# A new order of attention's steps, one softmax inverse a unit, and other places for the experts' first steps, in a fused attention and two-expert kernel

## The chip, the cores and the metric

The kernel runs on one core of a Trainium2 chip. The metric is the device time of one execution in microseconds. Three runs of the kernel before gave 928.98 us at the median (927.47 to 929.08).

## The reference, cut

Window attention over 4 batches, 8 heads, 576 positions and 64 columns a head, then two dense experts on 2304 rows of 512 columns.

```python
def _attn_ref(q, k, v):                         # (4, 8, 576, 64) each, float32
    scores = scale * np.matmul(q, k.transpose(0, 1, 3, 2))
    bias = slopes[:, None, None] * (-np.abs(rel).astype(np.float32))[None, :, :]
    mask = (rel >= 0) & (rel < window)          # window = 128
    scores = np.where(mask, scores + bias[None], -1000000000.0)
    scores = scores - np.max(scores, axis=-1, keepdims=True)
    attn = np.exp(scores)
    attn = attn / (np.sum(attn, axis=-1, keepdims=True) + 1e-09)
    return np.matmul(attn, v).astype(np.float32)

def _moe_ref(x, w_in, w_out, a, b):             # w_in (512, 2048), w_out (2048, 512)
    h = x @ w_in
    P = a[0] + a[1] * h + a[2] * h2 + a[3] * h3
    Q = 1.0 + np.abs(b[0]) * np.abs(h) + np.abs(b[1]) * h2
    return ((P / (Q + 1e-6)) @ w_out).astype(np.float32)

def _moe2_ref(x, w_in, w_out):
    h = x @ w_in
    return (np.where(h > 0.0, h, np.exp(np.minimum(h, 0.0)) - 1.0) @ w_out).astype(np.float32)
```

The weights of both experts come as 8-byte floats and are put together on the chip from their two 32-bit words.

## The kernel before, in words

**Units.** Attention runs over 16 units, `units[u] = (b, p)` with u = 4p + b: a batch b and a pair of heads p (e = 0, 1). A unit's 576 positions are four blocks of 128 and a tail of 64. Its work is cut into named steps:

- `qT`, `kT`, `zT`: TensorE transposes of q, of k and of the two tails; `qC`, `kC`, `zC`: their copies out of PSUM (`qC` on ScalarE, the others on VectorE).
- `S0` to `S4`: the scores on TensorE, five PSUM tiles a unit, taken in turn from three banks. `D0` to `D8`: nine VectorE instructions that add the bias and find the row's extreme. `E0` to `E8`: nine exponentials on ScalarE with the row's sum. `R0` and `R1`: the inverse of the sums (an add and a reciprocal each, over 5 and over 4 of the nine columns, line 523). `N0` to `N8`: the multiplication by the inverse on GpSimd.
- `T00`, `T10`, `T11`, `T01`: transposes of the probabilities, `C..` their copies on ScalarE. `V0`, `V1`, `Y`: the product with v. `XC` and `XY`: the copies of the result (128x512 and 128x64) into `xT`.
- `s`, `a`, `b`, `h`, `l` with 0 or 1: a weight's conversion, two weights in each of units 3 to 14 (`PLAN`, line 32): a scale on ScalarE, then a shift, a joining of the words, and the high and the low part on VectorE.

**The order.** `STEPS` (line 18) is a table written out by hand: each row is a step and how many iterations it runs ahead of (or behind) the loop's count t. The loop at line 667 goes through the table once an iteration and issues step by step, so the table sets the order on all engines' queues. Each engine runs its queue in order. A step that writes a buffer waits for the buffer's last readers. After the table's last row, three early iterations build the bias of the next head pair (`biases`, line 388, four VectorE instructions).

**The end of attention.** At iteration 15 `split_x` (line 217) splits the first 384 rows of `xT` into a high and a low part. From there on steps of the first expert stand between attention's: `early()` (line 264) gives the first products of the first four chunks (`gemm1`, 48 matmuls of 128x384, three at each `next`), at the places that `AHEAD` (line 34) names, and what is left runs after attention; `CONV_AFTER` (line 33) names six places for a step of the conversion of four more weights; `FIRST` (line 41) names where the elementwise part of chunks 0 and 1 stands (`rational`, line 269). The first product into the output accumulators (`gemm2_T(0)`, line 699) needs `ghi` and `glo` of chunk 0, which VectorE makes at lines 295 to 313.

**After attention** the first expert runs 96 chunks, each a `gemm1` and a `gemm2_T`, then the second expert. Nothing of that is changed.

## Time and profile before

| what | us |
| --- | --- |
| median of three runs (lowest, highest) | 928.98 (927.47, 929.08) |
| the profiled execution, its own time | 929.59 |
| its span, first to last instruction | 927.8 |
| busy: TensorE matmul, VectorE, ScalarE, GpSimd | 915.4, 795.9, 737.1, 185.0 |
| attention's unit in the middle of attention | 8.44 |
| first `gemm2_T` matmul that reads `glo`, from the span's start | 155.36 |

Times are read from the span's start. A timeline row has the start and the duration of an instruction (or of several in a row), its engine, line and tiles, and in brackets how long the engine stood idle before it and what ended that. On one engine the next row can begin before the last has ended, since instructions overlap at their ends; so what an instruction costs its engine is the distance from its start to the next start. Matmuls are pipelined, so a busy TensorE need not be at its peak.

### The profile page before, as it was taken

The page shows a single profiled execution, that of the slowest core. Times are in us where ns is not written, and L with a number is a line of the kernel's source. Part 1 is how long each engine was busy: PE and PEld are TensorE (multiplying, and loading weights), DVE is VectorE, ACT ScalarE, POOL GpSimd, SP SyncE. Part 2 cuts the span into 40 slices and gives each one's busy share as a digit, 9 for nine tenths or more (in the row PEclk, how much of TensorE's full clock was granted, in tenths as well). Part 3 has the DMA queues.
Part 4 walks back from the last instruction along what each step waited for, and adds up shares of the span by engine and source line. Part 5 has one row for each costly group of instructions (what it writes and reads, how often), then busy time and mean ns, then how long its engine had stood idle before and what let it go on. Part 6 is the DMA issues. An engine that isn't in the chain of part 4 may idle for free.

```text
span 927.8 us, 16722 instructions
## 1 busy us (share of the span) xinstructions
PE 915.4 (99%) x5494; PEld 839.2 (90%) x5494; DVE 795.9 (86%) x1873; ACT 737.1 (79%) x1614; POOL 185.0 (20%) x260
## 2 busy tenths in 40 slices
PE   8999999999999999999999999999999999999998
PEld 5776778999999999999999998888989898988887
DVE  6899999998998998998989999999978688677653
ACT  6999997889888888889888987676776567767553
POOL 5666661122222222222222210000000000000000
PEclk9999999999999999999999999999999999999999
DMA  8899952011222222222200034445253323442201
GB/s 160 228 247 240 222 168 82 1 35 58 85 80 70 86 69 86 85 63 92 85 31 29 3 119 136 164 144 197 80 170 103 121 83 98 142 148 81 79 0 69
DMA packets 112567, 98.35 MB, mean 106 GB/s; under 512 B 62816, under 2 KB 86368, under 8 KB 112480
## 3 DMA queue, kind: packets, MB, share of 16 engines
q1 hardware_dynamic: 109936, 96.57, 35.4%
q10 hardware_dynamic: 2544, 0.72, 0.4%
q8 instruction: 43, 0.70, 0.3%
q14 instruction: 44, 0.36, 0.1%
HBM read 79.96 MB, written 17.30 MB: 105 GB/s over the span
## 4 chain that ended last, share of the span: by engine, by line
PE 79%; DVE 15%; DMA 2%; ACT 2%; issue 2%; DVEq 0%; ACTq 0%; SPq 0%
PE acc L932 21%; PE m L916 18%; PE acc L708 18%; PE h L254 18%; DVE pr_wi L502 1%; DVE cvt L146 1%; PE s_ps L476 1%; DVE pr_wo L502 1%; PE x L569 1%; DMA v<-in_v_dram 1%; DVE w_wi L160 1%; DVE qq L298 1%; DVE ghi L295 1%; DVE ee L316 1%; DVE qkT L445 1%
## 5 line engine op out<-in xcount | busy, mean ns | idle before, releaser
L254 PE MATMUL h<-xs,w_wi 128*128 128x384 f32 x1152 | 216.9, 335 | 0.3 <-DVE xs L227 0.2
L254 PEld LDWEIGHTS h<-xs,w_wi 128*128 128x128 f32 x1152 | 200.7, 188 | 1.6 <-DVE xs L230 0.7
L708 PE MATMUL acc<-ghi,w_wo 128*128 128x384 f32 x768 | 194.8, 334 | 0.0
L313 POOL TENSOR_TENSOR glo<-ee,rr 128x384 fp32r<-128x384 f32 x92 | 93.6, 1018 | 311.3 <-DVE ee L312 109.3
L708 PEld LDWEIGHTS acc<-ghi,w_wo 128*128 128x128 f32 x768 | 138.6, 188 | 0.3 <-issue 0.3
L708 PE MATMUL acc<-glo,w_wo 128*128 128x384 f32 x384 | 128.4, 334 | 1.1 <-DVE glo L313 1.1
L932 PE MATMUL acc<-op_wo,ghi 128*128 128x512 f32 x288 | 89.6, 392 | 0.0
L916 PE MATMUL m<-xo_wi,op_wi 128*128 128x384 f32 x336 | 77.2, 337 | 0.0
L916 PE MATMUL m<-xo_wo,op_wi 128*128 128x384 f32 x336 | 76.5, 335 | 0.0
L301 ACT ACTIVATE rr<-qq,c_q 128x384 f32<-128x384 f32 x96 | 59.1, 616 | 18.6 <-DVE qq L298 17.7
L708 PEld LDWEIGHTS acc<-glo,w_wo 128*128 128x128 f32 x384 | 72.1, 188 | 1.4 <-DVE glo L313 1.4
L978 ACT ACTIVATE oo<-qq 128x384 f32<-128x384 f32 x24 | 12.6, 524 | 73.8 <-DVE qq L972 73.8
L284 ACT ACTIVATE oo<-h,a_sb 128x384 f32<-128x384 f32 x96 | 67.9, 707 | 3.4 <-DVE h L315 3.2
L287 ACT ACTIVATE ee<-h,a_sb 128x384 f32<-128x384 f32 x96 | 67.6, 704 | 0.0
L298 DVE SCALAR_TENSOR_TENSOR qq<-h,b_abs,qa 128x384 f32<-128x384 f32 x92 | 56.1, 609 | 12.4 <-ACT qa L283 11.3
L916 PEld LDWEIGHTS m<-xo_wo,op_wi 128*128 128x128 f32 x336 | 60.8, 188 | 4.0
L295 DVE TENSOR_TENSOR ghi<-ee,rr 128x384 fp32r<-128x384 f32 x96 | 53.5, 557 | 12.2 <-ACT h L282 0.5
L316 DVE TENSOR_TENSOR ee<-ee,h 128x384 f32<-128x384 f32 x96 | 53.3, 555 | 10.4 <-DVE h L315 0.5
L932 PEld LDWEIGHTS acc<-op_wo,ghi 128*128 128x128 f32 x288 | 53.5, 188 | 8.9
L916 PEld LDWEIGHTS m<-xo_wi,op_wi 128*128 128x128 f32 x336 | 60.5, 188 | 0.0
L282 ACT ACTIVATE h<-h 128x384 f32<-128x384 f32 x96 | 46.3, 482 | 15.2 <-PE h L254 14.5
L972 DVE TENSOR_TENSOR ee<-ee,m 128x384 f32<-128x384 f32 x96 | 52.7, 549 | 5.1 <-PE m L916 4.9
(184 smaller groups left out, 2067.6 us busy)
## 6 DMA issues: line engine op xcount, KB each, us to landing
pair<-joined_wo SPq DMA_DIRECT2D x43, 256.0 KB, 2.6
raw_wo<-in_moe_w_out_dram SPq DMA_DIRECT2D x20, 512.0 KB, 4.8
raw_wi<-in_moe_w_in_dram SPq DMA_DIRECT2D x16, 512.0 KB, 4.4
half<-in_moe_w_in_dram SPq DMA_DIRECT2D x32, 256.0 KB, 2.7
two_wo<-joined_wi SPq DMA_DIRECT2D x32, 256.0 KB, 2.9
s<-sums SPq DMA_DIRECT2D x32, 256.0 KB, 2.7
half<-in_moe_w_out_dram SPq DMA_DIRECT2D x22, 256.0 KB, 2.8
v<-in_v_dram SPq DMA_DIRECT2D x32, 128.0 KB, 3.4
```

The source lines that it names most:

```text
L254: nc.tensor.matmul(h, lhsT=WT["wi", f][:, SEL[wp], kk * P:(kk + 1) * P], rhs=x[xp][kk], start=(kk == 0 and n == 0), stop=(kk == KD - 1 and ...
L284: nc.scalar.activation(out=oo, in_=h2, func=AF.Identity, scale=a_sb[:, 3:4], bias=a_sb[:, 1:2])
L287: nc.scalar.activation(out=ee, in_=h2, func=AF.Identity, scale=a_sb[:, 2:3], bias=a_sb[:, 0:1])
L295: nc.vector.tensor_tensor(out=hi, in0=ee0, in1=rr0, op=ALU.mult)
L298: nc.vector.scalar_tensor_tensor(out=qq, in0=h2, scalar=b_abs[:, 1:2], in1=qa, op0=ALU.mult, op1=ALU.add)
L301: nc.scalar.activation(out=rr, in_=qq, func=AF.Ln, bias=c_q)
L313: (nc.gpsimd if c > 4 else nc.vector).tensor_tensor(out=low, in0=ee0, in1=rr0, op=ALU.mult)
L316: nc.vector.tensor_tensor(out=ee, in0=ee, in1=h, op=ALU.add)
L708: nc.tensor.matmul(acc_t[d], lhsT=WT["wo", f][:, SEL[wp], d * P:(d + 1) * P], rhs=gt[SEL[xp]], start=(f == 0 and n == 0), stop=(f == KF - ...
L916: nc.tensor.matmul(out, lhsT=w[:, SEL[wp], c0:c0 + P], rhs=XO[q // NP2, nm, k][:, SEL[xp]], start=(k == 0 and n == 0), stop=(k == 1 and n ...
L932: nc.tensor.matmul(acc_t[T, t], lhsT=gt[SEL[xp]][:, t * P:(t + 1) * P], rhs=w[:, SEL[wp]], start=(first and n == 0), stop=(last and n == 2),)
L972: nc.vector.tensor_tensor(out=t, in0=R[q, x], in1=M[q, m], op=ALU.add)
```

## The change

1. `STEPS` is a new table: all steps stand in another order and with other leads. One `R` over all nine columns takes the place of `R0` and `R1`.
2. `x_copy` becomes two steps: `XC` copies on ScalarE when u is even, `XD` on VectorE when u is odd (and for the last three units, as before).
3. The loads of q, k and v of a later unit are issued when all steps that read the buffer have been issued, whichever is last.
4. `AT_END` takes the place of `AHEAD`, `CONV_AFTER` and `FIRST`: it lists after which step of which unit each first step of the expert stands: `xA`/`xD` the split of x, `g0` to `g7` six matmuls of `gemm1` each, `r0a` to `r1d` the parts of the elementwise work of chunks 0 and 1 (`first_rational`), `zs`, `za`, `zb`, `zh`, `zl` with 0 to 3 the conversion steps of four more weights.

```diff
 STEPS = (
-    ("T00", -1), ("a0", 1), ("l1", -1), ("C01", -1), ("S0", 1), ("S1", 1), ("C00", -1),
...
+    ("qT", 3), ("E2", 1), ("D3", 2), ("XC", -1), ("T11", 0), ("h0", 1), ("C10", 0), ("h1", 0),
...
+    ("b1", 1), ("E0", 2), ("C00", 1), ("T10", 1), ("XD", 0), ("N7", 1), ("D1", 3),
 )
+AT_END = {
+    ("E5", 15): "xA xD",
+    ("T11", 14): "g0",
+    ("T01", 14): "g1",
+    ("C01", 14): "zs0 r0a",
+    ("V1", 14): "g2",
+    ("XY", 14): "r0b",
+    ("T10", 15): "g3",
+    ("XD", 14): "r0d za0 za2 zb0 za3 zh0",
+    ("T01", 15): "g4",
+    ("C01", 15): "r1a",
+    ("V1", 15): "g5 g6 g7",
+    ("XY", 15): "zl0 r1b zs3 r1c r0c zs2 zs1",
+    ("XD", 15): "zb3 zh3 r1d zl3 za1 zb1 zb2 zh2 zh1 zl2 zl1",
+}
...
-CONV_AFTER = ((15, "E8"), (15, "R1"), (14, "V1"), (15, "T01"), (15, "T11"), (15, "V1"))
-AHEAD = {
-    (14, "T00"): 1, (14, "T10"): 1, (14, "T11"): 2, (14, "V0"): 1, (14, "V1"): 2, (14, "Y"): 1,
-}
...
-FIRST = {"r0": (14, "Y"), "r1": (15, "C11")}
...
+    def first_rational(c):
...
+        def a():
+            nc.scalar.activation(out=h2, in_=h, func=AF.Square)
+            nc.scalar.activation(out=qq, in_=h, func=AF.Abs, scale=b_abs[:, 0:1])
+            nc.scalar.activation(out=oo, in_=h2, func=AF.Identity, scale=a_sb[:, 3:4], bias=a_sb[:, 1:2])
+            nc.scalar.activation(out=ee, in_=h2, func=AF.Identity, scale=a_sb[:, 2:3], bias=a_sb[:, 0:1])
+
+        def b():
+            nc.vector.scalar_tensor_tensor(
+                out=qq, in0=h2, scalar=b_abs[:, 1:2], in1=qq, op0=ALU.mult, op1=ALU.add
+            )
+
+        def r():
+            nc.scalar.activation(out=rr, in_=qq, func=AF.Ln, bias=c_q)
+            nc.scalar.activation(out=rr, in_=rr, func=AF.Exp, scale=-1.0)
+
+        def d():
+            nc.vector.tensor_tensor(out=h, in0=oo, in1=h, op=ALU.mult)
+            nc.vector.tensor_tensor(out=ee, in0=ee, in1=h, op=ALU.add)
...
-            def x_copy(u):
-                b, p = units[u]
-                copy("D" if u > NU - 4 else ENG["XC"], xT[:, p, b * S:b * S + NF * P], x_t.pop(u).rearrange("p i c -> p (i c)"))
+            def x_copy(eng):
+                def run(u):
+                    if (eng == "D") == (u % 2 == 1 or u > NU - 4):
+                        b, p = units[u]
+                        copy(eng, xT[:, p, b * S:b * S + NF * P], x_t.pop(u).rearrange("p i c -> p (i c)"))
+                return run
...
-                "R0": inverse(0, 5), "R1": inverse(5, 2 * NF + 1),
-                "Y": attn_v_tail, "XC": x_copy, "XY": x_tail_copy(ENG["XY"]),
+                "R": inverse(0, 2 * NF + 1),
+                "Y": attn_v_tail, "XC": x_copy("A"), "XD": x_copy("D"), "XY": x_tail_copy(ENG["XY"]),
...
-                    if step == "zT":
+                    gone[u].add(step)
+                    if step in ("qT", "kT", "zT") and {"qT", "kT", "zT"} <= gone[u]:
...
-                    elif step == "Y":
+                    elif step in ("V0", "V1", "Y") and {"V0", "V1", "Y"} <= gone[u]:
...
-            for t in range(first, NU + 2):
+            lates = [late for _, late in STEPS]
+            for t in range(-max(lates), NU - min(lates)):
...
-                if t == NU - 1:
-                    x1[0] = split_x(0, at_home, nc.vector, "DADA")
-                    ahead = early()
                 for step, late in STEPS:
-                    run(step, t + late)
...
+                    u = t + late
+                    if 0 <= u < NU:
+                        run(step, u)
+                        for at_end in AT_END.get((step, u), "").split():
+                            end_step(at_end)
```

The order that comes of it, at three places. First VectorE in the middle of attention, before: the end of one unit's softmax (L502 is a `D` step: the main instruction and a read of its accumulator; L526 and L529 are the inverse, here `R1`; L146 is the `b` step of a weight; L445 from `ps_qk` is `kC`).

```order
L502 ISA pr_wo_108,qq_104<-s_ps,ee_99 128x128
L502 ISA qq_104 128x1
L502 ISA pr_wo_108,qq_104<-s_ps,ee_99 128x256
L502 ISA qq_104 128x1
L526 TENSOR_SCALAR qq_104<-qq_104 128x4
L529 RECIPROCAL qq_104<-qq_104 128x4
```

Now, at the border of two iterations of an odd t (L480 into `xT` from `x` is `XD`, L537 the `D` steps 1 and 3 of the next unit, L162 the two `h`, L144 the two `a`, L561 and L564 the one inverse):

```order
L480 COPY xT<-x 128x512
L537 ISA pr_wi_105,qq_104<-s_ps,h_96 128x128
L537 ISA qq_104 128x1
L537 ISA pr_wi_105,qq_104<-s_ps,h_96 128x256
L537 ISA qq_104 128x1
L162 CAST w_wi_1157<-cvt_1069 128x512
L162 CAST w_wo_1161<-cvt_1050 128x512
L144 TENSOR_SCALAR raw_wo_871<-raw_wo_871 128x512
L561 TENSOR_SCALAR qq_104<-qq_104 128x9
L564 RECIPROCAL qq_104<-qq_104 128x9
L144 TENSOR_SCALAR raw_wi_1004<-raw_wi_1004 128x512
```

The nine columns have one inverse, and a 128x512 copy has come to VectorE in every second unit.

Second, VectorE where attention ends, before: from the last unit's `XY` (L445 from `ty`) to `glo` of chunk 0 (L313).

```order
L154 CAST w_wo_2397<-cvt_2335 128x512
L160 TENSOR_TENSOR w_wo_2397<-cvt_2335,w_wo_2397 128x512
L445 COPY xT<-ty 128x64
L445 COPY xT<-x 128x512
L295 TENSOR_TENSOR ghi_2443<-ee_2313,rr_2316 128x384
L307 SCALAR_TENSOR_TENSOR qq_2314<-qq_2314,ghi_2443 128x384
L312 TENSOR_TENSOR ee_2313<-ee_2313,qq_2314 128x384
L313 TENSOR_TENSOR glo_2444<-ee_2313,rr_2316 128x384
```

Now the same stretch, in two pieces without a gap (L480 from `ty` is the last unit's `XY`, from `x` its `XD`; L340, L349 and L350 are `r1b` and `r1d`; L144, L154, L162, L168 are `a`, `b`, `h`, `l` of the four weights; L303 to L321 make `ghi` and `glo` of chunk 0):

```order
L480 COPY xT<-ty 128x64
L168 TENSOR_TENSOR w_wi_2298<-cvt_2224,w_wi_2298 128x512
L340 SCALAR_TENSOR_TENSOR qq_2326<-h_2324,b_abs,qq_2326 128x384
L480 COPY xT<-x 128x512
L154 SCALAR_TENSOR_TENSOR cvt_2378<-cvt_2378,raw_wo_2014 128x512
L162 CAST w_wo_2390<-cvt_2378 128x512
L349 TENSOR_TENSOR h<-oo,h 128x384
L350 TENSOR_TENSOR ee_2325<-ee_2325,h 128x384
L168 TENSOR_TENSOR w_wo_2390<-cvt_2378,w_wo_2390 128x512
```

```order
L144 TENSOR_SCALAR raw_wo_2010<-raw_wo_2010 128x512
L154 SCALAR_TENSOR_TENSOR cvt_2386<-cvt_2386,raw_wo_2010 128x512
L154 SCALAR_TENSOR_TENSOR cvt_2384<-cvt_2384,raw_wi_2012 128x512
L162 CAST w_wi_2398<-cvt_2384 128x512
L162 CAST w_wo_2400<-cvt_2386 128x512
L168 TENSOR_TENSOR w_wi_2398<-cvt_2384,w_wi_2398 128x512
L168 TENSOR_TENSOR w_wo_2400<-cvt_2386,w_wo_2400 128x512
L303 TENSOR_TENSOR ghi_2411<-ee_2227,rr_2230 128x384
L315 SCALAR_TENSOR_TENSOR qq_2228<-qq_2228,ghi_2411 128x384
L320 TENSOR_TENSOR ee_2227<-ee_2227,qq_2228 128x384
L321 TENSOR_TENSOR glo_2412<-ee_2227,rr_2230 128x384
```

Between the last `XY` and `ghi` stood one instruction; now fifteen stand there.

Third, TensorE at the same place, before: the last unit's product with v (L569, L580), the `gemm1` matmuls that are left (L254), the first of `gemm2_T(0)` (L708).

```order
L569 MATMUL x<-pT,v_89 64x128 x14
L580 MATMUL ty<-pT,v_89 64x64 x4
L254 MATMUL h<-xs_2204,w_wi_876 128x384 x5
L254 MATMUL h<-xs_2205,w_wi_876 128x384 x4
L254 MATMUL h<-xs_2206,w_wi_876 128x384 x3
L254 MATMUL h<-xs_2204,w_wi_1014 128x384 x5
L254 MATMUL h<-xs_2205,w_wi_1014 128x384 x4
L254 MATMUL h<-xs_2206,w_wi_1014 128x384 x3
L708 MATMUL acc<-ghi_2443,w_wo_716 128x384 x2
```

Now (L604 and L615 are `V` and `Y`, L262 `gemm1`, L792 `gemm2_T`):

```order
L262 MATMUL h<-xs_2155,w_wi_885 128x384 x5
L262 MATMUL h<-xs_2156,w_wi_885 128x384
L604 MATMUL x<-pT,v_89 64x128 x6
L615 MATMUL ty<-pT,v_89 64x64 x4
L604 MATMUL x<-pT,v_89 64x128 x8
L262 MATMUL h<-xs_2156,w_wi_885 128x384 x3
L262 MATMUL h<-xs_2157,w_wi_885 128x384 x3
L262 MATMUL h<-xs_2155,w_wi_1021 128x384 x5
L262 MATMUL h<-xs_2156,w_wi_1021 128x384 x4
L262 MATMUL h<-xs_2157,w_wi_1021 128x384 x3
L792 MATMUL acc<-ghi_2411,w_wo_753 128x384 x2
```

Eighteen matmuls of `gemm1` stand between attention's last product and `gemm2_T(0)` where 24 stood, and `Y` now stands ahead of `V1`.

## Rows read from the trace of the kernel before

**Rows 1.** Windows: stretch, its length, busy PE, PEld, DVE, ACT, POOL, granted clock, DMA.

```profile
42.20:51.48 9.28, 8.35 (x86) 6.08 (x84) 8.86 (x36) 9.28 (x31) 5.58 (x9) 1.00 0.90 220
51.48:127.00 75.52, 73.48 (x746) 54.56 (x742) 74.93 (x296) 74.47 (x233) 50.14 (x81) 1.00 0.93 227
...
131.16:155.36 24.20, 21.64 (x197) 18.16 (x196) 22.82 (x61) 18.79 (x47) 8.69 (x14) 1.00 0.35 104
...
157.20:600.00 442.80, 442.49 (x2514) 436.96 (x2514) 404.34 (x842) 384.67 (x759) 93.61 (x92) 1.00 0.22 71
```

**Rows 2.** Timeline, VectorE in a middle unit: start, duration, engine, line, tiles.

```profile
81.75 0.16 DVE L526 TENSOR_SCALAR qq<-qq 128x4 f32<-128x4 f32 x1
...
82.04 0.66 DVE L146 SCALAR_TENSOR_TENSOR cvt<-cvt,raw_wi 128x512 int32<-128x512 int32 x1
...
84.58 0.32 DVE L526 TENSOR_SCALAR qq<-qq 128x5 f32<-128x5 f32 x1
...
85.04 0.39 DVE L154 CAST w_wo<-cvt 128x512 fp32r<-128x512 f32 x1
```

**Rows 3.** Timeline, ScalarE in the same unit: the copy of the result.

```profile
77.46 0.62 ACT L443 ACTIVATE xT<-x 128x512 f32<-128x512 f32 x1
```

**Rows 4.** Timeline, VectorE: bias of the second head pair, then `D4` of units 5 and 14.

```profile
13.59 0.42 DVE L391 SCALAR_TENSOR_TENSOR bias_wo<-relmask_wi 128x256 f32<-128x256 f32 x1
...
15.05 0.29 DVE L502 CUSTOM_DVE_ANT_0 pr_wi<-s_ps,bias_wo 128x128 f32<-128x128 f32 x1
...
47.63 0.41 DVE L502 CUSTOM_DVE_ANT_0 pr_wo<-s_ps,bias_wo 128x256 f32<-128x256 f32 x1
...
123.59 0.41 DVE L502 CUSTOM_DVE_ANT_0 pr_wo<-s_ps,ee 128x256 f32<-128x256 f32 x1
```

**Rows 5.** Timeline, VectorE at attention's end, from unit 15's `D4` to `ghi`.

```profile
131.16 0.41 DVE L502 CUSTOM_DVE_ANT_0 pr_wo<-s_ps,ee 128x256 f32<-128x256 f32 x1
...
147.42 0.42 DVE L154 CAST w_wi<-cvt 128x512 fp32r<-128x512 f32 x1
147.76 0.44 DVE L136 TENSOR_SCALAR raw_wo<-raw_wo 128x512 int32<-128x512 int32 x1
148.30 0.70 DVE L146 SCALAR_TENSOR_TENSOR cvt<-cvt,raw_wo 128x512 int32<-128x512 int32 x1
148.91 0.69 DVE L160 TENSOR_TENSOR w_wi<-cvt,w_wi 128x512 fp32r<-128x512 f32 x1
149.51 0.62 DVE L298 SCALAR_TENSOR_TENSOR qq<-h,b_abs,qq 128x384 f32<-128x384 f32 x1
...
151.18 0.42 DVE L154 CAST w_wo<-cvt 128x512 fp32r<-128x512 f32 x1
...
152.25 0.22 DVE L445 COPY xT<-ty 128x64 f32<-128x64 f32 x1
152.38 0.68 DVE L445 COPY xT<-x 128x512 f32<-128x512 f32 x1
152.98 0.55 DVE L295 TENSOR_TENSOR ghi<-ee,rr 128x384 fp32r<-128x384 f32 x1
```

**Rows 6.** Timeline, TensorE at attention's end.

```profile
131.63 1.13 PE L476 MATMUL s_ps<-qkT 64*128 64x256 f32 x6 [0.46 <-DVE qq L502]
...
146.01 1.03 PE L550 MATMUL ps_pT<-ident,pr_wo 128*128 128x128 f32 x7 [0.70 <-ACT pT L443]
...
149.25 4.45 PE L254 MATMUL h<-xs,w_wi 128*128 128x384 f32 x24
...
155.36 0.44 PE L708 MATMUL acc<-glo,w_wo 128*128 128x384 f32 x1 [1.10 <-DVE glo L313]
```

**Rows 7.** Windows of one us: columns as in Rows 1.

```profile
15.00:16.00 1.00, 0.25 (x1) 0.25 (x2) 0.97 (x8) 0.55 (x3) 0.72 (x2) 1.00 0.64 145
...
18.00:19.00 1.00, 1.00 (x5) 0.91 (x5) 0.94 (x5) 0.44 (x2) 1.00 (x3) 0.50 0.93 213
...
154.00:155.00 1.00, 0.26 (x2) 0.00 (x0) 0.93 (x3) 0.25 (x1) 0.00 (x0) 1.00 0.00 0
```

More of the change, by code (lines that the diff above doesn't have):

```diff
@@ L316, in rational @@
             nc.vector.tensor_tensor(out=ee, in0=ee, in1=h, op=ALU.add)
+    def first_rational(c):
+        h = h_t.pop(c)
+        h2, ee, qq, oo, rr = row("h2"), row(f"ee{c % 2}"), row(f"qq{c % 2}"), row("oo"), row(f"rr{c % 2}")
+        q_t[c] = (qq, ee, rr)
+        def a():
[13 more added lines that the diff above has]
+            nc.vector.tensor_tensor(out=ee, in0=ee, in1=h, op=ALU.add)
+        return {f"r{c}a": a, f"r{c}b": b, f"r{c}c": r, f"r{c}d": d}
     def attention():
@@ L432, in qk_tail_T @@
                 for n, nm in enumerate("qk"):
-                    _, r = raw_t.pop((nm, u))
+                    _, r = raw_t[nm, u]
                     nc.tensor.transpose(
@@ L561, in run @@
                     vr = raw_t["v", u]
-                    if i0 == 0:
+                    if u not in x_t:
                         x_t[u] = bank(3, [P, NF, P], "x")
@@ L576, in attn_v_tail @@
             def attn_v_tail(u):
-                vr = raw_t.pop(("v", u))
+                vr = raw_t["v", u]
                 for j in (NF - 1, NF):
@@ L611, in attention, with first_x, first_lo, first_parts @@
             CONV = {"s": conv_scale, "a": conv_shift, "b": conv_or, "h": conv_hi, "l": conv_lo}
+            gone = [set() for _ in range(NU)]
+            def first_x(c, eng):
+                for c in c:
+                    hi, _ = at_home(c)
+                    src = xT[:, c, 0:TB]
+                    if eng == "D":
+                        nc.vector.tensor_copy(hi, src)
+                    else:
+                        nc.scalar.activation(out=hi, in_=src, func=AF.Copy)
+            def first_lo(c):
+                hi, lo = at_home(c)
+                nc.vector.tensor_tensor(out=lo, in0=xT[:, c, 0:TB], in1=hi.bitcast(F32), op=ALU.subtract)
+            def first_parts():
+                for c in range(KD):
+                    if c % 2 == 0:
+                        first_x((c,), "D")
+                    first_lo(c)
+            x1[0] = {"hi": [], "lo": []}
+            ahead = early()
+            halves = {}
+            def end_step(step):
+                if step == "xA":
+                    for c in range(KD):
+                        hi, lo = at_home(c)
+                        x1[0]["hi"].append(hi)
+                        x1[0]["lo"].append(lo)
+                    first_x((1, 3), "A")
+                elif step == "xD":
+                    first_parts()
+                elif step[0] == "g":
+                    next(ahead, None)
+                    next(ahead, None)
+                elif step[0] == "r":
+                    c = int(step[1])
+                    if step[2] == "a":
+                        halves.update(first_rational(c))
+                    halves[step]()
+                else:
+                    key = order[24 + int(step[2])]
+                    if step[1] == "s":
+                        to_conv.remove(key)
+                        conv_scale(key)
+                    elif step[1] == "h":
+                        conv_hi(key, "D")
+                    elif step[1] == "l":
+                        conv_lo(key, "D")
+                    else:
+                        {"a": conv_shift, "b": conv_or}[step[1]](key)
             def run(step, u):
@@ L664, in load_some @@
                     load_w(to_load.pop(0))
-            first = -max(late for _, late in STEPS)
-            for t in range(first, NU + 2):
+            lates = [late for _, late in STEPS]
+            for t in range(-max(lates), NU - min(lates)):
                 if 0 <= t < 12:
                     load_some(2)
-                if t == NU - 1:
-                    x1[0] = split_x(0, at_home, nc.vector, "DADA")
-                    ahead = early()
                 for step, late in STEPS:
-                    run(step, t + late)
-                    if t < NU - 1 or not 0 <= t + late < NU:
-                        continue
-                    for _ in range(AHEAD.get((t + late, step), 0)):
-                        next(ahead, None)
-                    if (t + late, step) in CONV_AFTER:
-                        conv_step(to_conv, to_conv[0] not in LATE[4:], eng="D")
-                    if (t + late, step) == FIRST["r0"]:
-                        rational(0)
-                    if (t + late, step) == FIRST["r1"]:
-                        rational(1, old=False)
+                    u = t + late
[3 more added lines that the diff above has]
+                            end_step(at_end)
                 if -1 <= t < NP - 2:
```

2 lines of the change are left out of this document (1 added, 1 removed), and 15 rows, old and new, of the table STEPS.

## The prediction, on record before the run

> **What bounds the kernel now.** I read the windows first, stage by stage, then the timelines of the two stages that the change touches. From 157.20 on the experts keep TensorE busy 442.49 of 442.80 us, and nothing there is changed [rows 1]. So the change is worth what it moves the first `gemm2_T` matmul that reads `glo`, at 155.36 [rows 6]. In the nine middle units (75.52 us) VectorE is busy 74.93, ScalarE 74.47, TensorE 73.48 [rows 1]: VectorE bounds, ScalarE is right behind it, and no engine has 2.1 us to spare. At attention's end TensorE runs out of work first: it has 24 `gemm1` matmuls at 149.25 and then waits 1.10 us for `glo` [rows 6], while VectorE works through its queue without a gap [rows 5].
>
> I cut the time at the start of `D4`, a step that both kernels have once a unit: unit 5 at 47.63, unit 14 at 123.59 [rows 4], unit 15 at 131.16 [rows 5]. Units 5 to 14 take 75.96, 8.44 each; 14 to 15 takes 7.57; from unit 15's `D4`, called m below, to the `glo` matmul is 24.20.
>
> **Middle units.** Before, the inverse over 4 columns holds VectorE from 81.75 to 82.04, 0.29, and that over 5 from 84.58 to 85.04, 0.46 [rows 2]: 0.75. One over nine columns is not in the trace. Its two parts work on nine numbers a row, so it lies between the cheaper pair and the dearer one, 0.29 to 0.46; I take 0.30, since the dearer pair differs by a first part of 0.32 us, 0.16 in the other, for one column more, which is waiting and not work. That saves 0.45 a unit. `XD` brings a 128x512 copy to VectorE in odd units: 152.38 to 152.98, 0.60 [rows 5], on average 0.30 a unit. Net -0.15, so 8.29 a unit, alternately about 8.0 and 8.6. ScalarE gives a copy of up to 0.62 [rows 3] in odd units; it is not the bound, so this counts nothing, but it is what keeps ScalarE behind VectorE at the shorter period. Nine units: **-1.3**. The bounds: -2.0 if ScalarE's relief also takes away the 0.59 us that VectorE stands idle over the nine units (75.52 less 74.93 [rows 1]); +1.1 if the inverse costs the dearer 0.46 and odd units run 0.24 late with no even unit making it up.
>
> All other steps of the middle are the same instructions in another order. The loads of q, k and v go out at other places of SP's queue, none later against its reader than before; the DMA share there is 0.93 at 227 GB/s [rows 1], and a 2% shorter period asks 232. I cost that at nothing; if a load came late, TensorE's transposes would be late by its delay, once a unit. GpSimd is busy 50.14 of 75.52 [rows 1] and keeps its nine multiplications: nothing, save for rival 4.
>
> **Start, up to unit 5.** For: the first scores now stand ahead of the next unit's q transposes, so that the first `D` starts some 0.5 earlier (an estimate from the matmuls moved), and the unit from 42.20 to 51.48, which took 9.28 [rows 1], could fall back to the period, 0.84 less: -1.3. Against: the single inverse must wait for all nine exponentials; and the bias of a head pair, 13.59 to 15.05, 1.46 [rows 4], which is built at an iteration's border in three early iterations, now stands between `D1` and `D3` of one unit. `D3` frees the PSUM bank that `S2` or `S3` needs, so TensorE may wait about a third of it, 0.5, three times: +1.5. I take **-0.3**, nearer the gain since VectorE, not TensorE, is the fuller engine. The step from unit 14 to 15 I put at **+0.1** (its copy stays on VectorE as before, the order differs).
>
> **The end, from m on.** This is the largest term. TensorE ends attention at 149.25, m+18.09 [rows 6]. After: less scores behind `D4` (`S4` instead of six matmuls of 1.06 at 131.63), about -0.6; the waits of 0.46 and 0.70 [rows 6] mostly go, since a `gemm1` piece stands there now, -0.9; six more `gemm1` matmuls stand ahead (24 cost 4.45, so 0.185 each [rows 6]), +1.1. So m+17.7. `Y` stands before `V1` (1.0) now, so the last `XY` can start near m+16.9. VectorE without a stall would be there at about m+12.4: of the 24.20 it is busy 22.82 [rows 1], the work is the same after, and 10.4 of it now lies from `XY` on. So VectorE stalls there for some 4.5 us.
>
> Behind `XY` stand fifteen instructions before `ghi`, one stood there before. In distances from start to start [rows 5]: four `l` at 0.60 (148.91 to 149.51), three `b` at 0.61 (148.30 to 148.91), three `h` at 0.34 (147.42 to 147.76), one `a` at 0.54 (147.76 to 148.30), `r1b` and `r1d` 1.67 (149.51 to 151.18), `XD` 0.60: 2.4 + 1.8 + 1.0 + 0.5 + 1.7 + 0.6 = 8.0. With `XY`'s 0.13 (152.25 to 152.38) and the 2.38 from `ghi` at 152.98 [rows 5] to the matmul at 155.36 [rows 6], `glo`'s matmul comes at m + 16.9 + 0.13 + 8.0 + 2.4 = m+27.4, against m+24.20: **+3.2**. Bounds: -1.4, if VectorE never stalls and all its idle time goes; +4, if `Y` is a further 0.8 late. TensorE has only `V1` (1.0) and 18 matmuls (3.3) to lay over the 10.5 us: it stands idle for some 4.8 us ahead of `ghi`, and 1.2 more ahead of `glo`.
>
> **The clock.** In the window 15 to 16 TensorE was busy 0.25 of the time, and in 18 to 19 the granted clock was 0.50, the 1.2 GHz level, though it was then busy throughout. At 154 to 155 it was busy 0.26, and the clock stayed at 1.00, 2.4 GHz [rows 7]. An idle stretch of 4.8 us goes beyond both; I take the fall. There the windows stayed near 0.50 for some 3.2 us, of which [rows 7] shows one; half of that time is lost, and a fall at the end would cost the same: **+1.6** (0 to 1.7).
>
> The Trainium skill, "TensorE: Matmul & The Clock Gate", section "Part 1: The HAM clock gate", says that the slow clock is the default and that activity releases it. The fall after the window 15 to 16 agrees with that; the window 154 to 155 shows that not every gap costs the clock. By that rule an idle TensorE goes back to the low level and my sum stands; by the window at 154 alone the sum would be 1.6 less, as in rival 2.
>
> **Sum.** -0.3 - 1.3 + 0.1 + 3.2 + 1.6 = +3.3. The profiled execution took 929.59, so 932.9 there; the median of the runs is 0.6 lower: **932.3**.
>
> **Rivals.**
> 1. VectorE never stalls at the end (faster). Then the new order only saves work: -0.3 - 1.3 + 0.1 - 1.4 = -2.9, 926.1 on the median. It needs the last `Y` 4.5 us earlier than I have it. For it: TensorE's work for unit 15 is short, and most of the time up to 149.25 is other units' and `gemm1` matmuls that could have been placed behind. Against: the order does not place them behind. 15%.
> 2. The clock holds over the gap: 932.3 - 1.6 = 930.7. For it stands the window at 154 [rows 7]. 20%.
> 3. Attention gains more than I count, by its better bounds (-1.3 at the start, -2.0 in the middle): 1.7 less, 930.6. For it: ScalarE, second fullest, is relieved too. 12%.
> 4. The single inverse comes too late (slower still). GpSimd's multiplications of a unit can begin only once it ends, and TensorE's first transposes wait for five of them. I count 0.8 us of slack a unit (the fifth ends some 1.9 us after a unit's `D4`, the transposes stand some 2.7 after it: estimates from the new order and the durations in the middle); from there on, each 0.1 us on GpSimd lengthens every unit. At 0.5 a unit over nine units +4.5: 936.8. For it: GpSimd has no slot in which it can run ahead any more. Against: it is busy two thirds of the time [rows 1]. 9%.
>
> My forecast has the other 44%.
>
> **How the numbers follow.** A measurement of this kernel tells about 0.2%, 1.9 us, from no change: faster is below 927.1, slower above 930.8. Rival 1 is faster: 0.15. Rivals 2 and 3 lie at the border; with their spread some four fifths of them are within: 0.27. The rest, 0.58, is slower. The likeliest case alone runs from 930.5 to 934.5, by the bounds of the start and of the end. The range reaches to rival 1 and stops short of rival 4: 925.9 to 935.6.
>
> **What would show it.** Right: `D4` to `D4` of 8.3 in the middle, alternating by half a us; one inverse of 128x9 a unit at 0.30 to its successor; VectorE waiting for TensorE ahead of the last `XY` for 2 to 4 us; TensorE idle some 4.8 us ahead of the first `gemm2_T`, a granted clock of 0.50 in the windows after it; the `glo` matmul at 157 to 158. Wrong: no wait ahead of that `XY`, a `Y` that ends before m+14; units longer than 8.44, with TensorE waiting for GpSimd; a full clock throughout.

## The result, and the profile after

| | before | after |
| --- | --- | --- |
| median (lowest, highest), us | 928.38 (927.47, 929.08) | 934.55 (933.81, 936.50) |
| the profiled execution, own time | 929.59 | 933.81 |
| its span | 927.8 | 932.1 |
| `D4` of unit 5, 14, 15 | 47.63, 123.59, 131.16 | 47.25, 123.43, 131.06 |
| first matmul that reads `glo` | 155.36 | 158.06 |

The ratio is 1.0068, 95% interval 1.0055 to 1.0081: slower, as forecast (932.3, range 925.9 to 935.6). The medians stand 6.2 us apart, the profiled executions 4.2. Before's profiled execution is 1.2 above its median, because TensorE's clock fell in it early, which most executions of that kernel don't show (mean granted clock 0.998 in it, 1.000 in most others); more on that below. The spans are split at the same marks as in the prediction:

| stretch | forecast | measured in the profiles |
| --- | --- | --- |
| start to `D4` of unit 5 | -0.3 | -0.38 |
| nine units, to `D4` of unit 14 | -1.3 | +0.22 (76.18 against 75.96) |
| unit 14 to 15 | +0.1 | +0.06 (7.63 against 7.57) |
| unit 15's `D4` to the `glo` matmul | +3.2 | +2.80 (27.00 against 24.20) |
| from there to the end of the span | +1.6 | +1.6 (774.0 against 772.4; spans are read to 0.1) |
| sum | +3.3 | +4.3 |

**The end.** VectorE's timeline of the kernel after, with the rows that answer to [rows 5].

```profile
131.06 0.42 DVE L537 CUSTOM_DVE_ANT_0 pr_wo<-s_ps,ee 128x256 f32<-128x256 f32 x1
...
140.29 0.22 DVE L480 COPY xT<-ty 128x64 f32<-128x64 f32 x1 [0.88 <-PE ty L615]
...
147.35 0.22 DVE L480 COPY xT<-ty 128x64 f32<-128x64 f32 x1 [2.04 <-PE ty L615]
147.49 0.68 DVE L168 TENSOR_TENSOR w_wi<-cvt,w_wi 128x512 fp32r<-128x512 f32 x1
148.09 0.61 DVE L340 SCALAR_TENSOR_TENSOR qq<-h,b_abs,qq 128x384 f32<-128x384 f32 x1
148.62 0.68 DVE L480 COPY xT<-x 128x512 f32<-128x512 f32 x1
...
155.07 0.68 DVE L168 TENSOR_TENSOR w_wo<-cvt,w_wo 128x512 fp32r<-128x512 f32 x1
155.67 0.55 DVE L303 TENSOR_TENSOR ghi<-ee,rr 128x384 fp32r<-128x384 f32 x1
```

VectorE waits 0.88 for the last `XY` but one and 2.04 for the last, and then needs from 147.49 to 155.67, 8.2 us, for the fifteen instructions. TensorE, as [rows 6]:

```profile
148.10 3.42 PE L262 MATMUL h<-xs,w_wi 128*128 128x384 f32 x18
156.37 0.98 PE L792 MATMUL acc<-ghi,w_wo 128*128 128x384 f32 x2 [4.85 <-DVE ghi L303]
158.06 0.69 PE L792 MATMUL acc<-glo,w_wo 128*128 128x384 f32 x1 [0.71 <-DVE glo L321]
```

It stands idle 4.85 us ahead of `ghi` and 0.71 ahead of `glo`. Its clock, in windows as in [rows 7] (length, busy PE, PEld, DVE, ACT, POOL, granted clock, DMA):

```profile
155.00:156.00 1.00, 0.00 (x0) 0.00 (x0) 1.00 (x3) 0.00 (x0) 0.00 (x0) 1.00 0.02 8
156.00:157.00 1.00, 0.63 (x2) 0.50 (x2) 0.93 (x3) 0.00 (x0) 0.00 (x0) 0.56 0.00 0
...
161.00:162.00 1.00, 1.00 (x4) 1.00 (x4) 0.79 (x3) 1.00 (x3) 0.00 (x0) 0.50 0.00 0
162.00:163.00 1.00, 1.00 (x4) 1.00 (x4) 1.00 (x3) 0.89 (x2) 0.00 (x0) 0.52 0.00 0
163.00:164.00 1.00, 1.00 (x7) 1.00 (x7) 0.96 (x2) 0.95 (x2) 0.00 (x0) 1.00 0.00 0
```

After the gap the clock is at 0.50 (1.2 GHz) until about 163.

**The middle.** An even unit takes 7.98 and an odd one 8.57, as forecast, but two units are longer: 5 to 6 takes 9.46 and 8 to 9 takes 8.51. VectorE's waits from 47 to 131 lie in these two (engine, tile and line, what it waited for: us in total, times, longest; before had none there):

```profile
DVE raw_wi L144 <- DMA raw_wi<-in_moe_w_in_dram: 0.8, 2, 0.5
DVE pr_wi L537 <- PE s_ps L511: 0.2, 1, 0.2
```

The first of the two waits, with the load it waits for on SP's queue:

```profile
55.16 0.43 DVE L144 TENSOR_SCALAR raw_wi<-raw_wi 128x512 int32<-128x512 int32 x1 [0.55 <-DMA raw_wi<-in_moe_w_in_dram]
```

```profile
50.12 0.59 SPq L118 DMA_DIRECT2D raw_wi<-in_moe_w_in_dram  x1
```

Paired over the whole of attention, a unit's `raw_wi` load is issued 4.1 to 5.6 us ahead of the shift that reads it first (the last one 10.2); before it was 6.8 to 9.6. It took 4.1 to 5.0 us to land in the stretch from 36 to 60. The loads still go out at the head of an iteration, but the iteration begins at another point of a unit, and the table has `a0`, the shift of the first weight, at a lead of 2 instead of 1. `raw_wo`, read by `a1`, has more lead than before (11.0 to 12.8 against 7.2 to 9.9). The waits sum to 1.0, and the two units are 1.4 longer than others of their kind; what made up the rest was not followed.

### The profile page after: what moved, and what is told of

Same layout as the page of the kernel before. It is cut to its first block, busy times and chain, and to the rows that moved or that the text cites. A ratio compares the mean times of both kernels' runs of the same rounds, so it can differ in the third digit from the quotient of the medians.

```text
span 932.1 us, 16650 instructions
## 1 busy us (share of the span) xinstructions
PE 911.1 (98%) x5494; PEld 838.5 (90%) x5494; DVE 793.5 (85%) x1847; ACT 734.2 (79%) x1608; POOL 172.5 (19%) x260
## 4 chain that ended last, share of the span: by engine, by line
PE 90%; DVE 6%; ACT 1%; DMA 1%; issue 1%; POOL 0%; SPq 0%; DVEq 0%; POOLq 0%
PE h L262 21%; PE acc L792 21%; PE acc L1016 21%; PE m L1000 18%; PE s_ps L511 2%; PE ps_pT L585 2%; PE x L604 2%; DVE pr_wo L537 1%; DVE pr_wi L537 1%; PE ps_qk L455 1%; PE s_ps L493 1%; DVE cvt L154 1%; PE warm L743 0%; DVE qkT L480 0%; DMA raw_wi<-in_moe_w_in_dram 0%
## 5 line engine op out<-in xcount | busy, mean ns | idle before, releaser
L262 PE MATMUL h<-xs,w_wi 128*128 128x384 f32 x1152 | 216.8, 335 | 0.0
L262 PEld LDWEIGHTS h<-xs,w_wi 128*128 128x128 f32 x1152 | 201.6, 189 | 0.3 <-issue 0.3
L792 PE MATMUL acc<-ghi,w_wo 128*128 128x384 f32 x768 | 196.4, 336 | 4.8 <-DVE ghi L303 4.8
L321 POOL TENSOR_TENSOR glo<-ee,rr 128x384 fp32r<-128x384 f32 x92 | 93.5, 1016 | 316.3 <-DVE ee L320 117.8
L792 PEld LDWEIGHTS acc<-ghi,w_wo 128*128 128x128 f32 x768 | 139.6, 189 | 5.1 <-issue 5.1
L792 PE MATMUL acc<-glo,w_wo 128*128 128x384 f32 x384 | 129.2, 337 | 0.7 <-DVE glo L321 0.7
L792 PEld LDWEIGHTS acc<-glo,w_wo 128*128 128x128 f32 x384 | 72.6, 189 | 1.2 <-DVE glo L321 1.2
L303 DVE TENSOR_TENSOR ghi<-ee,rr 128x384 fp32r<-128x384 f32 x96 | 53.6, 558 | 11.9
L324 DVE TENSOR_TENSOR ee<-ee,h 128x384 f32<-128x384 f32 x94 | 52.1, 554 | 10.2 <-ACT xs L237 0.5
```

The costliest lines, as they stand in the source:

```text
L262: nc.tensor.matmul(h, lhsT=WT["wi", f][:, SEL[wp], kk * P:(kk + 1) * P], rhs=x[xp][kk], start=(kk == 0 and n == 0), stop=(kk == KD - 1 and ...
L303: nc.vector.tensor_tensor(out=hi, in0=ee0, in1=rr0, op=ALU.mult)
L321: (nc.gpsimd if c > 4 else nc.vector).tensor_tensor(out=low, in0=ee0, in1=rr0, op=ALU.mult)
L324: nc.vector.tensor_tensor(out=ee, in0=ee, in1=h, op=ALU.add)
L792: nc.tensor.matmul(acc_t[d], lhsT=WT["wo", f][:, SEL[wp], d * P:(d + 1) * P], rhs=gt[SEL[xp]], start=(f == 0 and n == 0), stop=(f == KF - ...
```

## Experiments

Kernels named e1 to e9 by their labels. Theory at the outset: the loss is the end (VectorE's wait and the fifteen instructions behind it) and the clock that falls in the gap, and the middle would gain if its loads were there. The rivals: that the place of VectorE's work at the end makes no difference, as it is the same work; that the clock costs nothing; that DMA, and not the order of its loads, is what is short.

**e7_before_behind: the end's order alone, in the kernel before.**

```diff
-CONV_AFTER = ((15, "E8"), (15, "R1"), (14, "V1"), (15, "T01"), (15, "T11"), (15, "V1"))
+CONV_AFTER = 6 * ((15, "XY"),)
```

> The kernel before with its six conversion steps at attention's end all standing behind the last XY, instead of spread ahead of it. Theory (VectorE then waits at XY for TensorE and does that work late): VectorE waits 3 us or more ahead of XY, the glo matmul comes 4 to 6 us later than 155.36, the clock falls to 0.50 after it, and the time is 932.5 to 935.5 against 928.4. Rival (the place of these steps makes no difference, since VectorE has the same work either way): 928.4.

Measured: 936.4, ratio 1.0090 (1.0074 to 1.0105), above the expected 935.5. By this alone the kernel before loses as much as the change does at its end, and more: `glo` came at 160.71, 30.94 behind unit 15's `D4` against 24.20, after 7.11 us of idle TensorE.

```profile
159.02 0.98 PE L708 MATMUL acc<-ghi,w_wo 128*128 128x384 f32 x2 [7.11 <-DVE ghi L295]
```

```profile
146.89 0.62 DVE L298 SCALAR_TENSOR_TENSOR qq<-h,b_abs,qq 128x384 f32<-128x384 f32 x1 [3.64 <-ACT qq L283]
```

The place of the steps matters, by 6.7 us here; the mechanism was not all as expected, though: of VectorE's idle time 1.4 us was at unit 14's `XY` and 4.9 us ahead of the elementwise work of chunks 0 and 1 (3.64 the longer wait), for ScalarE, and none at the last `XY`. VectorE had been emptied of work, so it waited for whichever engine came next.

**e1_fill: the clock alone.**

```diff
             run_all(ahead)
+            fill = bank(3, [P, PC], "fill")
+            w0 = WT["wi", 0]
+            for _ in range(18):
+                nc.tensor.matmul(fill, lhsT=w0[:, 0, 0:P], rhs=w0[:, 0], start=True, stop=True)
```

> The changed kernel with 18 matmuls of 128x512 into a free PSUM bank, behind the last gemm1 matmul, whose result nobody reads: they lie over most of the 4.85 us for which TensorE stands idle ahead of ghi. Theory (the gap costs the clock): the granted clock stays at 1.00 in the windows from 156 to 162, the glo matmul stays near 158.1, and what follows it is some 1.6 us shorter: about 932.9 against 934.55. Rival (VectorE sets the pace of the first chunks, the clock costs nothing there): the clock stays up and the time does not move, 934.5.

Measured: 931.8, ratio 1.0038 (1.0023 to 1.0053). That is 2.7 below the changed kernel and more than the 1.6 us, but not all of it is the clock: in its profile no load came late in the nine units (74.97 instead of 76.18). Whether loads were late in its other executions is not known. The part behind `glo` took 773.42 (931.0 less 157.58) against 774.04 and, before, 772.44. The 18 matmuls took the gap down to 0.64 and held the clock over it, yet in the profiled execution it fell a little later, for half as long:

```profile
154.00:155.00 1.00, 1.00 (x6) 0.62 (x4) 1.00 (x3) 0.00 (x0) 0.00 (x0) 1.00 0.00 0
155.00:156.00 1.00, 0.36 (x2) 0.20 (x2) 0.96 (x3) 0.00 (x0) 0.00 (x0) 1.00 0.02 8
156.00:157.00 1.00, 0.42 (x2) 0.10 (x1) 0.93 (x3) 0.03 (x1) 0.00 (x0) 1.00 0.00 0
157.00:158.00 1.00, 0.42 (x2) 0.42 (x3) 1.00 (x3) 1.00 (x2) 0.00 (x0) 0.93 0.00 0
158.00:159.00 1.00, 1.00 (x5) 1.00 (x4) 0.99 (x2) 1.00 (x3) 0.00 (x0) 0.50 0.00 0
...
161.00:162.00 1.00, 1.00 (x6) 1.00 (x6) 0.90 (x3) 1.00 (x3) 0.00 (x0) 0.86 0.00 0
```

The other three executions have a mean granted clock of 0.999 to 1.000 where this one has 0.998, and are 0.9 to 1.1 us shorter (931.63 to 931.89 against 932.75). The part behind `glo` gives the same 1.0 (773.42 against before's 772.44). So a fall at this place costs some 1.0 by the end of the span for 3.4 us of low clock (these windows) and 1.6 for 6.8 us (the changed kernel's). The rival, that it costs nothing, is out.

**e2_loads: the load alone.**

```diff
+                if t == 0:
+                    load_some(1)
                 if 0 <= t < 12:
-                    load_some(2)
+                    load_some(2 if t < 11 else 1)
```

> The changed kernel with the load of each unit's first weight (raw_wi) issued one iteration earlier, nothing else. Theory (VectorE's waits of 0.55 and 0.24 for raw_wi come from loads issued only 4 to 5.6 us ahead of their reader): both waits go, unit 5's D4 to unit 14's takes 74.8 instead of 76.17, the time is 1.2 to 2 us less, 932.5 to 933.3. Rival (the 16 DMA engines are the limit, 0.90 busy there): the wait moves to another load, and the nine units stay near 76.2, 934.5.

Measured: 932.56, ratio 1.0044 (1.0029 to 1.0059), 2.0 below the changed kernel. Both waits are gone, the units take 8.60 and 7.99 by turns, and nine of them 74.97:

```profile
47.29:122.26 74.97, 69.87 (x740) 53.71 (x738) 74.66 (x285) 73.33 (x232) 43.14 (x82) 1.00 1.00 236
```

That is 1.0 less than before's 75.96: the middle does gain what the copies and the inverse said, once its loads are in time. The expected 74.8 was nearly met, and 932.5 to 933.3 was. The rival is out: the wait did not move to another load, though the DMA share is 1.00 here, and 1.20 in the unit from 89.08 to 97.08, which takes its 8.00 all the same.

**e4_two_inv: two inverses side by side**, on top of e2_loads.

```diff
-("R", 1),
+("R0", 1), ("R1", 1),
-                "R": inverse(0, 2 * NF + 1),
+                "R0": inverse(0, 5), "R1": inverse(5, 2 * NF + 1),
```

> The kernel of e2_loads with two inverses again, over 5 and over 4 columns, one right behind the other where the one over nine columns stands. Theory (VectorE bounds the units, and an inverse costs by its instructions, not its columns): each unit is 0.3 to 0.5 longer, the nine units take 77.7 to 79.5 instead of 74.97, the time is 936 to 939 against e2_loads' 932.56. Rival (the two more instructions are small and overlap): the nine units within 0.5 of 74.97, 932.5 to 933.

Measured: 936.51, ratio 1.0085 (1.0071 to 1.0099); nine units 77.35 against 74.97, 0.26 each, a little under the expected 77.7; the time is within. A step of two small instructions, 128x4, costs 2.4 us over nine units and 3.9 in the time, as VectorE has no idle time to hide it in (busy 74.66 of e2_loads' 74.97).

```profile
63.11 0.15 DVE L561 TENSOR_SCALAR qq<-qq 128x5 f32<-128x5 f32 x1
63.30 0.19 DVE L564 RECIPROCAL qq<-qq 128x5 f32<-128x5 f32 x1
63.40 0.13 DVE L561 TENSOR_SCALAR qq<-qq 128x4 f32<-128x4 f32 x1
63.56 0.18 DVE L564 RECIPROCAL qq<-qq 128x4 f32<-128x4 f32 x1
63.66 0.40 DVE L144 TENSOR_SCALAR raw_wi<-raw_wi 128x512 int32<-128x512 int32 x1
```

**e3_copies: no copy on VectorE**, on top of e2_loads.

```diff
-if (eng == "D") == (u % 2 == 1 or u > NU - 4):
+if (eng == "D") == (u > NU - 4):
```

> The kernel of e2_loads with all 128x512 copies of the result on ScalarE again (but those of the last three units). In e2_loads an odd unit takes 8.60 and an even one 7.99, and ScalarE is busy some 73.6 us of the nine units' 74.97. Theory (VectorE bounds, ScalarE is right behind it): VectorE's 0.60 in five odd units go, but five copies of 0.48 more take ScalarE to some 76.0, and it becomes the bound: the nine units take 75.5 to 76.5 and the time is 933 to 934.5 against e2_loads' 932.56. Rival (VectorE alone counts, the copies cost nothing on ScalarE): all units take 7.99, the nine units 72.0, the time is 929 to 930.

Measured: 931.65, ratio 1.0039 (1.0024 to 1.0054), 0.9 below e2_loads; nine units 73.24. Neither case: four of the nine units take 7.99 to 8.01, as the rival had it, the others 8.08 to 8.61. So the copies on VectorE cost 1.7 us in the middle, of which 0.9 arrives in the time, and do not pay.

```profile
47.37:120.61 73.24, 71.88 (x739) 53.45 (x738) 72.11 (x280) 73.24 (x235) 43.17 (x82) 1.00 1.00 243
112.00:120.61 8.61, 8.59 (x87) 6.43 (x86) 8.05 (x32) 8.61 (x30) 4.79 (x10) 1.00 0.99 271
```

ScalarE is busy 73.24 of 73.24, with five copies more no longer than in e2_loads (73.33). My error: I added the copies to a busy time that had slack in it, since instructions that overlap here share their time. Nor does the full share make ScalarE the bound. It is full in the units of 7.99 too, and in e9_best, which has all these copies on ScalarE as well, five units in a row take 8.00, this one the last of them:

```profile
112.05:120.05 8.00, 7.82 (x82) 5.67 (x81) 7.97 (x34) 8.00 (x27) 4.80 (x10) 1.00 0.95 273
```

What stretches e3_copies' later units stays open. In the longest TensorE is busy 8.59 of 8.61, and its weight load for the product with v waits 0.26 us for a load of v.

**e8_bias: the start**, on top of e2_loads. `biases(t + 2)` is issued ahead of the last step of the table, `D1`, and not behind it.

```diff
                 for step, late in STEPS:
                     u = t + late
+                    if (step, late) == STEPS[-1] and -1 <= t < NP - 2:
+                        biases(t + 2)
...
-                if -1 <= t < NP - 2:
-                    biases(t + 2)
```

> The kernel of e2_loads with one move: in the three early iterations VectorE builds the bias of the next head pair ahead of the last D1 instead of behind it. Theory (in the start TensorE and VectorE wait for each other by turns: VectorE waits 4.8 us in all for the scores that D1 reads, and D1's follower D3, which gives the bank back, then stands behind the 1.4 us of bias work): the bias work falls into VectorE's waits ahead of D1, and unit 5's D4 comes 1.5 to 2.5 us before e2_loads' 47.29, so 930 to 931 against 932.56. Rival (the start goes by TensorE, 3.8 of 4 us busy in its windows, and the bias work is hidden): unit 5's D4 within 0.5 us of 47.29, 932 to 933.

Measured: 931.72, ratio 1.0036 (1.0023 to 1.0049). `D4` of unit 5 came at 45.11, 2.18 earlier, as the theory had it; but of the 2.2 only 0.8 arrived in the median, which lies between the two cases. The unit behind it took 9.61 in place of 8.60, as a load of v came 0.83 late. Its DMA share was 1.05; units of e2_loads with more had no late load, so the share alone does not explain it:

```profile
47.23 1.22 PE L604 MATMUL x<-pT,v 128*64 128x128 f32 x11 [0.83 <-DMA v<-in_v_dram]
```

```profile
45.11:54.72 9.61, 8.41 (x84) 6.10 (x82) 8.75 (x33) 8.80 (x28) 4.79 (x10) 1.00 1.05 234
```

**e5_end: the order of the end.** Two weights are converted ahead of the last `XY`, the steps of two more are put off to behind chunk 0's `glo`.

```diff
...
-    ("XD", 14): "r0d za0 za2 zb0 za3 zh0",
+    ("XD", 14): "r0d za0 zb0 zh0 zl0 za3 za2",
+    ("C10", 15): "zs3",
-    ("T01", 15): "g4",
+    ("T01", 15): "g4 zb3 zh3 zl3",
...
-    ("XY", 15): "zl0 r1b zs3 r1c r0c zs2 zs1",
-    ("XD", 15): "zb3 zh3 r1d zl3 za1 zb1 zb2 zh2 zh1 zl2 zl1",
+    ("XY", 15): "r1b r1c",
+    ("XD", 15): "r1d later",
...
+                    for s in "zb2 zh2 zl2 za1 zb1 zh1 zl1".split():
+                        put_off.append(lambda s=s: end_step(s))
```

> The changed kernel with another order at attention's end only: two of the four weights are converted ahead of the last XY, in VectorE's idle time, the steps of the other two stand behind chunk 0's glo, between the steps of chunks 1 and 2; r0c stands right behind r0b. Behind the last XY stand then four instructions ahead of ghi instead of fifteen. Theory: the glo matmul comes at 152.5 to 153.5 instead of 158.06, the clock stays at 1.00, and the time is some 6 us less than 934.55, 928 to 929. Rival (the work behind glo comes back as waits of TensorE in chunks 0 to 4): glo as early, but 3 to 4 us are given back ahead of chunk 5, 931 to 932.5.

Measured: 930.45, ratio 1.0020 (1.0009 to 1.0031). `glo` came 21.70 behind unit 15's `D4` instead of 27.00, at full clock. But the part behind `glo` took 775.5 (929.9 less 154.38), 3.1 more than before's: the rival's 3 to 4, though the time lies between the two cases. TensorE waits for `glo` in chunks 0, 2 and 4:

```profile
154.38 0.45 PE L797 MATMUL acc<-glo,w_wo 128*128 128x384 f32 x1 [0.89 <-DVE glo L322]
...
164.48 0.44 PE L797 MATMUL acc<-glo,w_wo 128*128 128x384 f32 x1 [1.51 <-DVE glo L322]
...
174.13 0.45 PE L797 MATMUL acc<-glo,w_wo 128*128 128x384 f32 x1 [1.05 <-POOL glo L322]
```

The seven instructions that were put off are some 3.6 us of VectorE's work (by the distances of the prediction), and most of that came back. (The total gains 4.1 on the changed kernel all the same, even with 2.6 us of load waits in its profile, as it has e2_loads' fault.) So VectorE's work, from the middle of attention to the first chunks, is one stretch: moving work along it gains what idle time it fills and no more.

**e6_best: less work for VectorE at the end.** With e2_loads' load; the shifts and joins, but one weight's join, ahead of the last `XY`; the casts (`h`) of the four weights on ScalarE, their low parts (`l`) on GpSimd. Both had room: in the changed kernel they were busy 18.57 and 8.72 of the 27.00 us from unit 15's `D4` to `glo`.

```diff
...
+    ("XD", 14): "r0d za0 zb0 za3 za2",
+    ("C10", 15): "zs3 zh0 zl0",
+    ("T01", 15): "g4 zb3 za1",
+    ("C01", 15): "zs2 r1a zh3 zl3",
+    ("V0", 15): "zb2",
...
+    ("XY", 15): "r1b r1c zs1 zh2 zl2",
+    ("XD", 15): "r1d later",
...
-                        conv_hi(key, "D")
+                        conv_hi(key, "A")
...
-                        conv_lo(key, "D")
+                        conv_lo(key, "G")
```

> The changed kernel with the earlier load of raw_wi (as e2_loads) and an end at which VectorE has less to do: of the four weights converted there the high parts are cast on ScalarE and the low parts computed on GpSimd, the shifts and joins stand ahead of the last XY in VectorE's idle time, and one weight's join is left for behind chunk 0's glo. Theory (VectorE's work from the middle of attention to the first chunks sets the time, so what is taken off it there is not given back): the nine units at 75.0, unit 15's D4 near 129.9, the glo matmul some 21 to 22 us behind it, at 151 to 152, full clock, no wait of TensorE over 0.5 in the chunks behind: 925 to 926.5, faster than the kernel before (928.3). Rival (the first chunks wait for VectorE as in e5_end): glo as early, but 2 to 3 us given back by chunk 5: 928 to 929.

Measured: 927.19, ratio 0.9989 (0.9980 to 0.9998): a little faster than the kernel before. `glo` comes at 152.69, 22.61 behind `D4`; behind it 772.8 us, so nearly nothing is given back. It missed the forecast 925 to 926.5 by 0.7: `glo` came 0.6 later behind `D4` than the 22 that I had at most, and TensorE still waits 1.84 for it; the end of this document tells which instructions were long there.

**e9_best: all of it.** e6_best with e8_bias and e3_copies, and the first low part on VectorE again.

> All of it together: e6_best with the bias work ahead of D1 (e8_bias), the copies of the result on ScalarE (e3_copies), and the first of the four low parts at the end on VectorE again, since in e6_best VectorE's neighbours of a GpSimd subtraction took 0.96 to 1.53 us instead of 0.42 to 0.56. Theory (each of the four places costs what it was measured to cost by itself): unit 5's D4 near 45.5, the nine units 73.2 to 73.8, unit 15's D4 near 126.5 to 127, the glo matmul 21.5 us behind, full clock: 921.5 to 924, faster than the kernel before by 0.4 to 0.7%. Rival (ScalarE, now busy all the time, is late at the end too, or the places add less than their sum): 925 to 927.

Measured: 926.65, ratio 0.9981 (0.9973 to 0.9990), the fastest of all, and short of its sum: the rival. Unit 5's `D4` is at 45.23 as expected, but the nine units take 74.82 and not 73.2 to 73.8: two of them take 9.3 and 9.2 in place of 8.0, and in these loads of v come 0.74 and 0.39 late, which is under half of what they lose. And from unit 15's `D4` at 127.70 to `glo` it is 23.91 in place of 22.61: TensorE waits 1.86 there for a copy of ScalarE, 0.94 in e6_best:

```profile
133.85 0.55 PE L587 MATMUL ps_pT<-ident,pr_wo 128*128 128x128 f32 x3 [1.86 <-ACT pT L480]
...
151.61 0.44 PE L800 MATMUL acc<-glo,w_wo 128*128 128x384 f32 x1 [1.88 <-DVE glo L323]
```

## Why the prediction was right, and where it was not

**What bounds the kernel: right.** The whole change was in the first 158 us, and VectorE bounds the middle: an instruction of 128x4 more or a copy less on it is seen in the period (e4_two_inv, e3_copies).

**The middle: the terms were right, the loads wrong.** -0.45 for the inverse and +0.60 for a copy in odd units gave 7.99 and 8.59; 7.99 and 8.60 were measured (e2_loads). One inverse took 0.33 to its successor, where I had 0.30. Two side by side took 0.29 and 0.26 (e4_two_inv) and lengthened a unit by 0.26; so some 0.2 of the 0.75 before was the wait that I had seen in the dearer pair, and the rest the second pair of instructions. I rounded to an average of 8.29 over nine units, but five of the nine hold a copy, so it is -1.0 and not -1.3. The step that failed is the sentence that the loads go out "none later against its reader than before", costed at nothing. I had looked at q, k and v only. The weights' loads stayed where they were while their readers moved: `raw_wi` lost some 3.5 us of its lead and came down to the time that it takes to land. That cost 1.2 us in this execution and made the middle +0.2. It differs from one execution to the next: e1_fill, with the same loads, has no such wait in its profile, e5_end has 2.6 us of them. Moving the load took 2.0 us off the median.

**The start: right by the profiles, wrong by what was in them.** -0.38 against -0.3. But before's profiled execution had lost time there to the clock: the windows 16 to 20 show a mean of 0.57, and the same code in e7_before_behind 1.00 (before, then e7_before_behind).

```profile
16.00:20.00 4.00, 4.00 (x19) 2.92 (x19) 3.87 (x19) 3.13 (x12) 2.87 (x7) 0.57 0.70 157
```

```profile
16.00:20.00 4.00, 3.91 (x31) 2.65 (x31) 3.93 (x23) 3.95 (x15) 3.18 (x7) 1.00 0.71 159
```

e7_before_behind, in which attention's order is before's, has its unit 5's `D4` at 46.31. Against that, the changed kernel's 47.25 is 0.9 later, and the sum by the terms would be 5.6, near the 6.2 of the medians. The mechanism that I named against the change, the bias work between `D1` and `D3`, is what costs: taken from there it gave 2.18 (e8_bias), and I had bounded it at +1.5. My choice of a value nearer the gain, since VectorE was the fuller engine, was wrong: in the changed kernel's start VectorE waits 5.6 us in all for scores, 2.0 before. The gain was there too: unit 0's `D4` comes at 9.52, against 10.10 in before's profile and 10.49 in e7_before_behind. So -0.3 was met because the clock's loss in before's profile hid a start that is slower, not for the forecast's reason: that is luck.

**The end: right, one term inside it wrong.** Forecast 27.4 from `D4` to `glo`, measured 27.00; `XY` at 16.29 behind `D4` (16.9), the way from there to `ghi` 8.32 (8.1), TensorE idle 4.85 (4.8). Of the 4.5 us that VectorE was to stall it stood idle 2.04 there and 0.88 at the `XY` before, 2.9: the `XY` came 0.6 earlier than I had it, and VectorE, whose work I had taken for the same 22.82, is busy 23.56.

```profile
131.06:158.06 27.00, 19.99 (x195) 17.55 (x195) 23.56 (x59) 18.57 (x45) 8.72 (x17) 0.96 0.29 93
```

Since the last `Y` sets the time at that point, this changed nothing. On TensorE the two waits of 0.46 and 0.70, which I let go for -0.9, grew:

```profile
131.54 0.54 PE L493 MATMUL s_ps<-qkT 64*64 64x192 f32 x4 [0.80 <-DVE qq L537]
...
136.00 0.55 PE L585 MATMUL ps_pT<-ident,pr_wo 128*128 128x128 f32 x3 [0.97 <-ACT pT L478]
```

Attention's last product still ended at 148.10, 17.04 behind `D4` and not 17.7, as the other matmuls of the stretch took less than I had counted. That the place of the last `Y` came out within 0.6 is in part luck.

**The clock: the fall right, its price by luck.** The clock fell behind the gap, to 0.50, and stayed there from 156 to 163, twice as long as I had taken it, and yet it cost the 1.6 that I had by halving 3.2 us. Two things made up for that. The first 1.9 us of the low stretch lie ahead of the `glo` matmul, where TensorE waits for VectorE anyway. The 4.9 us behind it cost nearly their half, from the `glo` matmul to the next chunk's first `gemm2_T` 6.16 us against 3.92, with TensorE busy throughout (before, then after):

```profile
155.36:159.28 3.92, 3.92 (x22) 3.92 (x23) 3.64 (x8) 3.89 (x8) 0.00 (x0) 1.00 0.00 0
```

```profile
158.06:164.22 6.16, 6.16 (x23) 6.16 (x23) 5.81 (x12) 5.94 (x11) 0.00 (x0) 0.60 0.00 0
```

Of these 2.24 us some 0.6 come back later in the span: before loses 0.28 in a `gemm1` at 207.12 that takes 2.52 instead of 2.24, and the rest was not followed. In e1_fill, whose 3.4 us of low clock lie wholly behind `glo`, the same distance is 5.52. The rule of the Trainium skill, "TensorE: Matmul & The Clock Gate", "Part 1: The HAM clock gate", that the slow clock is the default and activity releases it, agrees with these windows: busy 0.00 in 155 to 156, clock 0.56 in the next. Rival 2, the clock that holds, is out for this gap.

**The other rivals.** Rival 1 (no stall) did not happen. Rival 3 (attention gains more) neither. Rival 4 (the single inverse too late for GpSimd) neither: in the nine units TensorE's matmuls wait for VectorE alone (6.1 us in all), and with the loads in time the period is VectorE's own.

**The numbers.** 934.55 lies 2.2 above the forecast: some 1.2 for the start, 1.5 for the middle, less 0.4 at the end. The likeliest case's own range (930.5 to 934.5) just missed it; with the load moved (e2_loads) 932.56 lies in it.

## What to carry to other kernels

When steps are moved, pair each load with its first reader, those included that stand still in the text, and compare the lead with the time the load takes to land: a load that stays where it was becomes late when its reader moves ahead. Where one engine's work bounds a stretch, its idle time in it is the only thing an order can win; work that is put behind the next handover comes back there, and only work taken off the engine stays gone. Before you take a profiled execution as the measure, see that its own time is near the median, and search its windows for what it has that others may not. And a term that comes out on its number can be two errors that cancel: ask of each part of it whether an engine was waiting there anyway.
